# Waiting for the last zero fills on GpSimd instead of SyncE

## The chip, the cores and the metric

The kernel runs on one core of a Trainium2 chip. A core has five engines, each with its own instruction queue: TensorE (PE in the profile; its weight loads are PEld), VectorE (DVE), ScalarE (ACT), GpSimd (POOL) and SyncE (SP), which does not compute. SyncE, ScalarE and GpSimd issue the transfers, which 16 DMA engines carry out. Engines wait for each other and for transfers on semaphores. The metric is the device time of one execution in microseconds; lower is better.

## The reference

It is one decoder layer for one token with its backward pass: attention over a cached window, then a gated bilinear block, then the gradients of everything.

```python
W = min(4096, max(256, Sk // 4))                  # 4096 of Sk = 32768 cached rows
k = jnp.repeat(k_cache[:, :, Sk - W:, :], rep, axis=1)
v = jnp.repeat(v_cache[:, :, Sk - W:, :], rep, axis=1)
...
h = x + _A_ref(_layernorm(x, axis=-1), A_k_cache, A_v_cache, A_wq, A_wo)
h2 = h + _B_ref(_layernorm(h, axis=-1), B_w_gate, B_w_up, B_w_down)
...
_out, _vjp = jax.vjp(_f, A_x, A_k_cache, A_v_cache, A_wq, A_wo, B_w_gate, B_w_up, B_w_down)
_grads = _vjp(grad_out)
```

There are 8 key/value heads of 256 elements and 16 query heads. The gradients of the two caches (out_2 and out_3) have the full shape of the caches, 8 x 32768 x 256 in bfloat16, 134 MB each. Only the last 4096 rows of each head have a gradient; the 28,672 rows ahead of them are zero, and these zeros have to be written.

## The kernel before

The work has three stages. In the first, for each of the eight heads g, the kernel loads the window of keys and values, computes scores and softmax (`scores`) and sums of products (`moments`). The middle stage computes the output and the feed-forward block with its gradient. The last stage goes over the heads again in the order 6, 1, 3, 4, 5, 0, 7, 2 and computes the gradients of the window, which ScalarE's queue stores (L715); between the heads GpSimd computes the gradients of the weights (`outer`, L595, and `outer_B`, L632) and issues their stores. The last of these is the store of `job_qB` (L659), after which GpSimd has nothing but the program's end.

Beside this run the zero fills: 16 regions, one per head and cache, of 14,336 KB each (`regions`, L244). SyncE's queue (`ZQ`, L41) issues them. Two early ones read from the zeroed tile `pair` (L246); GpSimd waits for these (L248) before it loads over `pair`. The other 14 read from the tile `home` once VectorE has zeroed the rows that they use (`clear_rows`, L281). `fill_late` (L253) issues them, two at a time: a fill waits until the one before the last has landed, on one of two semaphores `zsem`. One region (`UNEVEN`) is split, and four of its pieces are issued by GpSimd, with a semaphore `psem` of their own. `fill_late` is called while head 1 of the first stage is traced (L401).

A framework called Tile orders each engine's instructions and sets the semaphores between them. The fills are kept out of its bookkeeping (`no_tile_sem_insts`, and the group "fills"), so the kernel waits for them itself: `fill_late` ends with waits of SyncE on `psem` and both `zsem` (L276 to L278), and the last of these waits is declared as the fence of the group (L279), the instruction that stands for the landing of all its members. `keep_in_program_order` pins an instruction behind what was traced before it on its engine.

When the context of the launch closes (L769), the program's end follows: SyncE waits for all semaphores of the framework, one instruction after another with up to two semaphores each, and drains; the other engines drain; GpSimd collects all of them in a barrier, clears the semaphores, and a second barrier ends the program.

Of the kernel before, what the change touches and what calls it, by code (L numbers as in the profile page):

```python
# [8 lines left out]
f32 = mybir.dt.float32  # L9
# [26 lines left out]
def kernel(  # L36
        ctx, tc, A_x, A_k_cache, A_v_cache, A_wq, A_wo, B_x, B_w_gate, B_w_up, B_w_down, grad_out,
           out_0, out_1, out_2, out_3, out_4, out_5, out_6, out_7, out_8):
    nc = tc.nc
    LD = nc.scalar  # L40
    ZQ = nc.sync  # L41

    const = ctx.enter_context(tc.tile_pool(name="const", bufs=1))
# [85 lines left out]
    nc.vector.memset(ones_bf[:], 1.0)  # L129
    ones_f = const.tile([128, 1], f32)  # L130
    nc.vector.memset(ones_f[:], 1.0)
    eps_t = const.tile([128, 1], f32)
    nc.vector.memset(eps_t[:], EPS)

# [66 lines left out]
    def load_kv(dst, cache, g, queue=LD):  # L201
        queue.dma_start(out=dst, in_=cache[0, g, Sk - W:, :].rearrange("(p t) d -> p t d", t=T))  # L202
# [32 lines left out]
    def rows_of(src, n):  # L235
        return src[0:128:4].unsqueeze(1).to_broadcast([32, n, src.shape[1]])

    def fill_with(dst, src, sem, group, queue=ZQ):
        fill = queue.dma_start(out=dst, in_=src)
        tc.info.no_tile_sem_insts.add(fill.ins.name)  # L240
        tc.add_to_no_dep_group(group, fill.ins)
        tc.keep_in_program_order(fill.then_inc(sem, 16))
# [10 lines left out]
    def fill_late():  # L253
        zsem = [tc.alloc_semaphore(f"zsem{j}") for j in range(DEEP)]
        psem = tc.alloc_semaphore("psem")
        due = [0] * DEEP
        for i, reg in enumerate(regions[EARLY:]):
            j = i % DEEP
            if i >= DEEP:
                tc.keep_in_program_order(ZQ.wait_ge(zsem[j], due[j]))  # L260
            n = NZ
            if i + EARLY == UNEVEN:
                odd = reg.rearrange("(r f) -> r f", f=ZW)[22 * 32:]
                reg = reg[0:22 * 32 * ZW]
                n = 22
                at = 0
                for e, base, rows, queue in ((3, 0, 8, nc.gpsimd), (2, 12, 2, nc.gpsimd), (3, 20, 13, nc.gpsimd), (8, 64, 13, nc.gpsimd), (4, 0, 5, ZQ), (1, 0, 1, ZQ)):
                    fill_with(odd[at:at + e * rows].rearrange("(e n) f -> e n f", e=e),
                              Z_late[base:base + 4 * e:4].unsqueeze(1).to_broadcast([e, rows, ZW]), zsem[j] if queue is ZQ else psem, "fills", queue)
                    at += e * rows  # L270
                    if queue is ZQ:
                        due[j] += 16
            for dst, src in [(reg.rearrange("(p n f) -> p n f", p=32, f=ZW), rows_of(Z_late, n))]:
                fill_with(dst, src, zsem[j], "fills")
                due[j] += 16
        tc.keep_in_program_order(ZQ.wait_ge(psem, 64))  # L276
        for j in range(DEEP):
            filled = tc.keep_in_program_order(ZQ.wait_ge(zsem[j], due[j]))  # L278
        tc.declare_fence(filled.ins, group="fills")  # L279

    def clear_rows():  # L281
        words = Z_late.bitcast(mybir.dt.int32)
        nc.vector.tensor_tensor(out=words, in0=words, in1=keep_i[:].to_broadcast([128, ZW // 2]), op=ALU.bitwise_and)
# [39 lines left out]
    with tc.tile_pool(name="ps_x", bufs=1, space=bass.MemoryType.PSUM) as ps_x, \  # L323
# [36 lines left out]
        def moments(g, p_f):  # L360
            K_sb, V_sb = K_of[g], V_of[g]
            if g < G - 1:
                M_t = ps_m.tile([128, 2, 2 * Dh], f32, tag="M", name="M_t")
                M_ps = [M_t[:, vh, :] for vh in range(2)]
            else:
                M_ps = [ps_tr.tile([128, 4, 128], f32, tag="tr", name="M_t")[:].rearrange("p t k -> p (t k)") for _ in range(2)]
            for c in range(8):
                pK = pK_slot[c % 2]
                for i in range(4):
                    t = 4 * c + i  # L370
                    for hh in range(2):
                        nc.vector.tensor_scalar(out=pK[:, i, hh, :], in0=K_sb[:, t, :], scalar1=p_f[:, 8 * i + c, hh:hh + 1], scalar2=None, op0=ALU.mult)  # L372
                for i in range(4):
                    t = 4 * c + i
                    for vh in range(2):
                        nc.tensor.matmul(M_ps[vh], lhsT=V_sb[:, t, vh * 128:(vh + 1) * 128], rhs=pK[:, i, :, :].rearrange("p h d -> p (h d)"),  # L376
                                         start=(t == 0), stop=(t == T - 1))
            for t in range(0, T, 4):
                for k in range(4):
                    tk, X_sb = t + 2 * (k // 2), (V_sb, K_sb)[k % 2]  # L380
                    nc.tensor.matmul(ok_ps[32 * k:32 * (k + 1), :], lhsT=ppad[g % 2][:, tk:tk + 2, :].rearrange("p t h -> p (t h)"),  # L381
                                     rhs=X_sb[:, tk:tk + 2, :].rearrange("p t d -> p (t d)"),
                                     start=(g == 0 and t == 0), stop=(g == G - 1 and t == T - 4))
            if g < G - 2:
                move_M(g, M_ps)
            else:
                M_late.append((g, M_ps))
# [7 lines left out]
        for g in range(G):  # L395
            p_f = p_next
            if g + 1 < G:
                p_next = scores(g + 1)
            if g == 1:
                clear_rows()  # L400
                fill_late()  # L401
            moments(g, p_f)
            for w, h in NEXT.get(g, ()):
                load_kv((K_of, V_of)[w][h], (A_k_cache, A_v_cache)[w], h)
            if g == G - 2:
                LD.dma_start(out=wo_sb[:, JW:], in_=wo_v[:, JW:])
                LD.dma_start(out=wd_sb, in_=wd_v[0])
# [23 lines left out]
    with tc.tile_pool(name="ps_mid", bufs=2, space=bass.MemoryType.PSUM) as ps_mid, \  # L431
# [76 lines left out]
        def close(dn, dcat):  # L508

            nc.vector.tensor_tensor(out=dn[:, 3:5], in0=dn[:, 3:5], in1=par_f[:], op=ALU.mult)  # L510
            nc.vector.tensor_copy(out=dcat[:, 0:3], in_=dn[:, 0:3])
            nc.vector.tensor_tensor(out=dcat[:, 3:4], in0=dn[:, 3:4], in1=dn[:, 4:5], op=ALU.add)
# [64 lines left out]
    with tc.tile_pool(name="work2", bufs=2) as work2, tc.tile_pool(name="lnw", bufs=1) as lnw, \  # L577
# [94 lines left out]
        for it, g in enumerate((6, 1, 3, 4, 5, 0, 7, 2)):  # L672
# [53 lines left out]
            if it == 6:  # L726
                dn1 = lnw.tile([128, 5], f32)
                for c, src, dq in ((0, wq2[0], dq_bc), (1, wq2[1], dq_bc), (2, wq2[2], dq_bc),
                                   (3, wqB, dq_bc[:, 0:HJ]), (4, wqB, dq_bc[:, HJ:2 * HJ])):
                    part = nc.vector.tensor_tensor_reduce(out=wq2[0][:, 0:src.shape[1]], in0=src, in1=dq, scale=1.0, scalar=0.0,  # L730
                                                          op0=ALU.mult, op1=ALU.add, accum_out=dn1[:, c:c + 1])
                    if c == 0:
                        tc.keep_in_program_order(part)
                dcat1 = lnw.tile([128, 8], f32)
                close(dn1, dcat1)
                dxT = layernorm_bwd(dcat1, xnT_f, rstd1, dhT[:], "ln1")
                dx_ps = ps_t.tile([1, D], f32, tag="tmp")
                for c in range(3):
                    nc.tensor.matmul(dx_ps[0:1, c * 128:(c + 1) * 128], lhsT=dxT[:, c:c + 1], rhs=ident_f[:], start=True, stop=True)
                nc.tensor.matmul(dx_ps[0:1, 384:D], lhsT=dxT[:, 3:4], rhs=pair_f[:], start=True, stop=True)  # L740
                dx_bf = x_bf
                nc.vector.tensor_copy(out=dx_bf[:, 0:384].rearrange("o (p c) -> o p c", c=3), in_=dx_ps[0:1, 0:384].rearrange("o (c p) -> o p c", c=3))
                nc.vector.tensor_copy(out=dx_bf[:, 384:D], in_=dx_ps[0:1, 384:D])
                LD.dma_start(out=out_1.rearrange("a b d -> (a b) d"), in_=dx_bf[:])

# [1 line left out]
_INS = ['A_x', 'A_k_cache', 'A_v_cache', 'A_wq', 'A_wo', 'B_x', 'B_w_gate', 'B_w_up', 'B_w_down', 'grad_out']  # L747
# [26 lines left out]
```

## Time and profile before

| | |
|---|---|
| median of 3 runs | 783.92 us (783.14 to 784.41) |
| the profiled execution: its time | 784.15 us |
| the profiled execution: span from first to last instruction | 782.4 us |
| bytes moved | 331.43 MB (50.43 MB read from HBM, 280.59 MB written to it) |
| mean rate over the span | 424 GB/s |
| busy share of PE, DVE, ACT, POOL | 57%, 49%, 25%, 24% |
| last issue of a fill by SyncE | 702.86 us |
| GpSimd's last issue (L659) | 682.97 us |
| ScalarE's last two stores (L715): start of the issues | 716.43 us |

The profile is one execution. Times count from the span's start. Digits in the page's slices are busy tenths of one fortieth of the span. A "q" behind an engine (SPq, POOLq) marks an instruction of its queue that waits, drains or issues and is not counted as busy. EVENT_SEMAPHORE is a wait on, or an update of, a semaphore; its start is the moment when the wait is over. DRAIN is the instruction with which an engine closes its work ahead of a barrier.

### The profile page before, as it was taken

The page shows a single profiled execution, that of the slowest core. Times are in us where ns is not written, and L with a number is a line of the kernel's source. Part 1 is how long each engine was busy: PE and PEld are TensorE (multiplying, and loading weights), DVE is VectorE, ACT ScalarE, POOL GpSimd, SP SyncE. Part 2 cuts the span into 40 slices and gives each one's busy share as a digit, 9 for nine tenths or more (in the row PEclk, how much of TensorE's full clock was granted, in tenths as well). Part 3 has the DMA queues.
Part 4 walks back from the last instruction along what each step waited for, and adds up shares of the span by engine and source line. Part 5 has one row for each costly group of instructions (what it writes and reads, how often), then busy time and mean ns, then how long its engine had stood idle before and what let it go on. Part 6 is the DMA issues. An engine that isn't in the chain of part 4 may idle for free.

```text
span 782.4 us, 6400 instructions
## 1 busy us (share of the span) xinstructions
PE 449.5 (57%) x2172; PEld 192.3 (25%) x2190; DVE 385.2 (49%) x1088; ACT 197.8 (25%) x309; POOL 190.2 (24%) x102
## 2 busy tenths in 40 slices
PE   1999999796889753313336985426888075021000
PEld 1444444242344321101122342112332031010000
DVE  8068655351178531142785284915675057964000
ACT  1442332334400000000111273405545045013000
POOL 7000001000000000000001977529194746900000
PEclk9999999899689956555557997556885567555555
DMA  9999999999999999999999999999999999999997
GB/s 375 431 420 431 427 436 417 426 430 427 431 428 423 427 428 429 430 429 430 432 432 433 428 426 427 427 410 428 432 415 427 417 431 432 430 431 426 430 428 327
DMA packets 23554, 331.43 MB, mean 424 GB/s; under 512 B 1758, under 2 KB 2786, under 8 KB 4802
## 3 DMA queue, kind: packets, MB, share of 16 engines
q1 hardware_dynamic: 14826, 250.43, 75.4%
q10 hardware_dynamic: 5176, 57.09, 17.2%
q0 software_dynamic: 3520, 23.51, 7.2%
q8 instruction: 17, 0.28, 0.1%
q14 instruction: 15, 0.12, 0.0%
HBM read 50.43 MB, written 280.59 MB: 423 GB/s over the span
## 4 chain that ended last, share of the span: by engine, by line
DMA 24%; PE 24%; DVE 18%; ACT 2%; issue 2%; DVEq 0%; ACTq 0%; POOLq 0%
DMA out_dram<-arena 11%; DMA arena<-in_B_w_up_dram 7%; DMA arena<-in_B_w_down_dram 4%; PE rows_ps L313 4%; PE M_t L376 4%; PE tr_ps L310 4%; PE d_ps L705 4%; DVE pair L730 3%; DMA arena<-in_A_k_cache_dram 2%; DVE arena L712 2%; DVE arena L713 2%; DVE arena L527 2%; PE dqb_ps L583 2%; DVE arena L471 2%; PE dqb_ps L589 1%
## 5 line engine op out<-in xcount | busy, mean ns | idle before, releaser
L372 DVE TENSOR_SCALAR arena<-arena,p_f 128x256 bf16<-128x256 bf16 x512 | 110.1, 280 | 34.1 <-PE tr_ps L310 16.1
L310 PE MATMUL tr_ps<-ident_f,arena 128*128 128x128 f32 x448 | 84.7, 319 | 44.7 <-DMA arena<-in_A_v_cache_dram 31.9
L313 PE MATMUL rows_ps<-arena,vpad 128*16 128x512 bf16 x256 | 88.9, 442 | 8.2 <-ACT arena L329 3.0
L329 ACT COPY arena<-tr_ps 128x1024 bf16<-128x1024 bf16 x64 | 63.6, 1013 | 83.8 <-PE tr_ps L310 82.1
L310 PEld LDWEIGHTS tr_ps<-ident_f,arena 128*128 128x128 f32 x448 | 56.2, 159 | 92.6 <-issue 64.5
L712 DVE CAST arena<-d_ps 128x512 bf16<-128x512 f32 x64 | 44.0, 688 | 67.3 <-PE d_ps L705 66.7
L376 PE MATMUL M_t<-arena 128*128 128x512 bf16 x308 | 75.2, 386 | 0.8 <-issue 0.2
L705 PE MATMUL d_ps<-arena 32*128 32x512 bf16 x256 | 46.8, 514 | 48.3 <-DVE arena L713 40.6
L709 ACT CAST arena<-d_ps 128x512 bf16<-128x512 f32 x64 | 37.9, 593 | 85.6 <-PE d_ps L705 81.7
L600 POOL TENSOR_SCALAR arena<-dh_bc,oX_f 128x448 bf16<-128x448 bf16 x32 | 44.9, 1412 | 28.8 <-DMA out_dram<-arena 28.6
L713 DVE CAST arena<-d_ps 128x512 bf16<-128x512 f32 x64 | 43.5, 680 | 13.8 <-DMA out_dram<-arena 13.8
L710 ACT CAST arena<-d_ps 128x512 bf16<-128x512 f32 x64 | 38.3, 599 | 23.8 <-DMA out_dram<-arena 23.8
L678 ACT COPY arena<-tr_ps 128x1024 bf16<-128x1024 bf16 x32 | 32.7, 1024 | 28.3 <-PE rows_ps L313 18.2
L376 PEld LDWEIGHTS <-arena 128*128 128x128 bf16 x320 | 30.2, 100 | 37.2 <-issue 7.1
L600 POOL TENSOR_SCALAR arena<-arena,xT 128x4096 bf16<-128x4096 bf16 x3 | 31.9, 10618 | 26.8 <-DMA out_dram<-arena 26.8
L315 DVE COPY arena<-rows_ps 16x512 f32<-16x512 f32 x16 | 10.8, 677 | 48.5 <-PE rows_ps L313 48.3
L417 POOL DMA_DIRECT2D arena<-in_A_wo_dram x1 | 0.6, 572 | 136.5 <-PE ok_ps L381 136.5
L482 PE MATMUL r_ps<-arena,X2pad 128*4 128x448 bf16 x24 | 10.4, 571 | 39.7 <-DMA arena<-in_B_w_up_dram 25.3
L600 POOL TENSOR_SCALAR arena<-pair,xT 128x1792 bf16<-128x1792 bf16 x6 | 28.7, 4794 | 12.7 <-DMA out_dram<-arena 12.6
L705 PEld LDWEIGHTS <-arena 32*128 32x128 bf16 x256 | 10.5, 96 | 86.8 <-DVE arena L713 41.8
L376 PE MATMUL M_t<-arena,pair 128*128 128x512 bf16 x124 | 29.5, 397 | 0.4 <-issue 0.2
L202 POOL DMA_DIRECT2D pair<-in_A_v_cache_dram x2 | 1.2, 629 | 114.5 <-POOLq L248 114.5
(240 smaller groups left out, 593.4 us busy)
## 6 DMA issues: line engine op xcount, KB each, us to landing
out_dram<-home SPq DMA_DIRECT2D x13, 14336.0 KB, 88.0
out_dram<-arena ACTq DMA_DIRECT2D x16, 2048.0 KB, 24.7
out_dram<-pair SPq DMA_DIRECT2D x2, 14336.0 KB, 93.5
out_dram<-home SPq DMA_DIRECT2D x1, 11264.0 KB
arena<-in_A_k_cache_dram ACTq DMA_DIRECT2D x5, 2048.0 KB, 21.5
arena<-in_A_k_cache_dram SPq DMA_DIRECT2D x3, 2048.0 KB, 19.7
arena<-in_A_v_cache_dram SPq DMA_DIRECT2D x3, 2048.0 KB, 30.0
arena<-in_A_v_cache_dram ACTq DMA_DIRECT2D x3, 2048.0 KB, 32.2
```

Of the source, the lines that this page charges most:

```text
L310: nc.tensor.transpose(tr_ps[:, i, :], X_sb[:, 4 * q + i, :].bitcast(f32), ident_f[:])
L313: nc.tensor.matmul(rows_ps[:], lhsT=pad[:, e, 16 * q:16 * q + 16], rhs=XT.rearrange("p (n e) -> p n e", e=2)[:, :, e], start=(q == 0 and e ...
L329: sT_ps = dots(K_of[g], KT_slot, vpad[g % 2], rows1, ps_c, "cols", lambda q, XT, ps: nc.scalar.copy(out=XT, in_=ps))
L372: nc.vector.tensor_scalar(out=pK[:, i, hh, :], in0=K_sb[:, t, :], scalar1=p_f[:, 8 * i + c, hh:hh + 1], scalar2=None, op0=ALU.mult)
L376: nc.tensor.matmul(M_ps[vh], lhsT=V_sb[:, t, vh * 128:(vh + 1) * 128], rhs=pK[:, i, :, :].rearrange("p h d -> p (h d)"), start=(t == 0), s ...
L600: nc.gpsimd.tensor_scalar(out=buf[:, off:off + n], in0=src, scalar1=col, scalar2=None, op0=ALU.mult)
L678: nc.scalar.copy(out=XT, in_=ps)
L705: nc.tensor.matmul(d_ps[:, qi].rearrange("p w d -> p (w d)"), lhsT=rm[32 * q:32 * (q + 1), l, :], rhs=Rs[32 * q:32 * (q + 1), :], start=Tr ...
L709: nc.scalar.copy(out=stV[:, t:t + 2, :], in_=d_ps[:, :, 0, :])
L710: nc.scalar.copy(out=stK[:, t:t + 2, :], in_=d_ps[:, :, 1, :])
L712: nc.vector.tensor_copy(out=stV[:, t:t + 2, :], in_=d_ps[:, :, 0, :])
L713: nc.vector.tensor_copy(out=stK[:, t:t + 2, :], in_=d_ps[:, :, 1, :])
```

## The change

A tile `done_t` of one element is added. `fill_late` no longer ends with the waits but returns its semaphores and the counts that they are to reach. A new function, `fills_done`, is called at the end of the kernel function, after all heads of the last stage. In it GpSimd waits on `psem` and both `zsem`, then sets `done_t` to zero, and this memset is declared as the fence. SyncE no longer waits for the last fills by an instruction of the kernel.

```diff
+    done_t = const.tile([1, 1], f32)
...
-        tc.keep_in_program_order(ZQ.wait_ge(psem, 64))
+        return zsem, psem, due
+
+    def fills_done(zsem, psem, due):
+        tc.keep_in_program_order(nc.gpsimd.wait_ge(psem, 64))
         for j in range(DEEP):
-            filled = tc.keep_in_program_order(ZQ.wait_ge(zsem[j], due[j]))
+            tc.keep_in_program_order(nc.gpsimd.wait_ge(zsem[j], due[j]))
+        filled = tc.keep_in_program_order(nc.gpsimd.memset(done_t[:], 0.0))
         tc.declare_fence(filled.ins, group="fills")
...
-                fill_late()
+                fill_sems = fill_late()
...
+        fills_done(*fill_sems)
```

## The prediction

> **What bounds the kernel now.** I read the page first, then the table by stretches of time, then SyncE's waits, then the instructions of the closing line. The page:
>
> ```profile
> span 782.4 us, 6400 instructions
> ...
> DMA  9999999999999999999999999999999999999997
> ...
> DMA packets 23554, 331.43 MB, mean 424 GB/s; under 512 B 1758, under 2 KB 2786, under 8 KB 4802
> ```
>
> The DMA engines are full in every slice but the last, while the busiest compute engine, PE, is busy for 57%. The kernel is 331.43 MB of transfers: 331.43 MB at 424 GB/s is 781.7 us, the whole span. So a change pays only if it moves bytes, or shortens what lies before the first or after the last of them. The end, by stretches (busy time and count of PE, PEld, DVE, ACT and POOL, then the clock, the DMA share and GB/s):
>
> ```profile
> 720.00:770.00 50.00, 0.00 (x0) 0.00 (x0) 0.00 (x0) 0.00 (x0) 0.00 (x0) 0.50 1.01 429
> 770.00:776.00 6.00, 0.00 (x0) 0.00 (x0) 0.00 (x0) 0.00 (x0) 0.00 (x0) 0.50 1.01 431
> 776.00:781.00 5.00, 0.00 (x0) 0.00 (x0) 0.00 (x0) 0.00 (x0) 0.00 (x0) 0.50 0.35 147
> 781.00:783.00 2.00, 0.00 (x0) 0.00 (x0) 0.00 (x0) 0.00 (x0) 0.00 (x0) 0.50 0.00 0
> ```
>
> From 720 us on no engine computes; the fills alone run, thin out from 776, and nothing moves after 781. What SyncE waits for, its last issue, and what runs on the program's closing line (duration in ns, then first and last start):
>
> ```profile
> SPq L239 <- DMA out_dram<-home: 576.7, 12, 76.7
> SPq L278 <- DMA out_dram<-home: 77.3, 2, 43.2
> ...
> 702.86 0.53 SPq L239 DMA_DIRECT2D out_dram<-home  x1
> ...
> L278 SPq EVENT_SEMAPHORE  x2: 17/22/28, 746.6 to 780.7; - x2
> ...
> L769 SPq EVENT_SEMAPHORE  x11: 17/28/28, 780.8 to 781.4; - x11
> L769 SPq DRAIN  x2: 7/10/13, 781.5 to 781.6; - x2
> ...
> L769 POOLq EVENT_SEMAPHORE  x2: 17/17/17, 781.6 to 781.7; - x2
> L769 POOLq DRAIN  x1: 18326/18326/18326, 682.9 to 682.9; - x1
> ```
>
> SyncE issues the last fill at 702.9, then stands in L278 until 780.7. Only then does it go through eleven waits and two drains (780.8 to 781.6), and GpSimd's barrier step at 781.6 follows them. GpSimd's own closing drain was over at 682.9 + 18.3 = 701.3; the drains of PE, DVE and ACT on that line started between 715.0 and 718.1. So between the last fill and the barrier only SyncE's list is on the path. The chain of waits on the page does not help here: it follows DVE's early drain and ends at 716.
>
> The views round these starts to a tenth; the trace's records hold them finer: last fill's semaphore 780.73, L278 released 780.74, first of the eleven waits 780.84, drains 781.51 and 781.57, GpSimd's step 781.60. So the path from last fill to barrier step is 0.87 us. Behind it stand the two barriers and GpSimd's clearing of semaphores (781.6 to 782.4), and 784.15 - 782.4 = 1.75 us outside the span; the change leaves both alone.
>
> **The change part by part.** The sum is made against the profiled execution, 784.15 us, which lies 0.23 above the median of 783.92 and inside the runs shown (783.14 to 784.41). I carry differences over to the median.
>
> *Removed from SyncE: the waits of L276 to L278.* Nothing but the closing line is queued behind them. Its eleven waits now run from about 703.4 on, while fills run for 77 us more: 780.74 to 781.51 leaves the path. Most of these waits are on semaphores long complete (the last store lands at 741.9); those not yet complete cost nothing before 780.
>
> *Added to GpSimd: the same waits and a memset of one element.* What is queued behind them is only GpSimd's closing drain and barrier steps: its last work is the issue at 683.0 (L659). No transfer and no other engine's work waits for that. All engines wait for GpSimd in the barrier, as before.
>
> *The new path from the last fill to GpSimd's barrier step.*
> - Release to memset: GpSimd operations that waited for a transfer (L600, L635) start 0.08 to 0.10 us after its semaphore by the records. If the last wait stays an instruction of its own, like L248 (17 ns), it is 0.02 more. I take 0.10.
> - The memset: four memsets at the start (L758) took 93 to 97 ns, the one of 128x128 283 ns. One element is nearest to the former: 0.09.
> - GpSimd's drain behind it: with nothing else in flight 40 and 113 ns here, 169 ns behind the four memsets, where it ended 0.05 after the last of them. It lies beside the next item: 0.
> - SyncE takes up the memset's count. In the records the drain at 781.51 is the instruction that names the semaphore of GpSimd's operations; none of the eleven waits does. So SyncE should stand in that drain already. A semaphore from one engine to another took 0.03 (SyncE's drain over at 781.58, GpSimd's step at 781.60), the second drain starts 0.06 after the first, and 0.03 again to GpSimd: 0.12 to 0.13.
>
> Sum 0.10 + 0.09 + 0.13 = 0.32 us, against 0.87: 0.55 us less. Profiled 783.6, at the median 783.4.
>
> Bounds of what the trace of before does not show. The shortest path is 0.08 + 0.09 + 0.12 = 0.29, a gain of 0.58. At the other end GpSimd's drain after the fills: the one of 18.3 us ended at 701.3, 1.1 us after its transfer landed (issue 682.97, 17.2 us to landing); if that 1.1 is always paid once GpSimd has issued transfers, the path is 0.10 + 0.09 + 1.12 + 0.04 = 1.35, 0.48 slower than now. I take the short drain, as nothing is in flight on GpSimd by 781.
>
> The Trainium skill's page "VectorE: DVE Perf Modes", section "The DRAIN you can't avoid", holds that the drains of the program's frame take a constant 12 ns or so on all five engines. This trace agrees for SyncE (7 to 13 ns) and not for GpSimd (40 to 18,326 ns). By that page the drain costs 0.01 instead of 0.05, beside the same 0.13 of SyncE, and the sum stays 0.32; by the long row it would be the first slow rival below, so the page speaks against that rival and the row keeps it alive.
>
> *done_t* takes four bytes per partition and moves the small tiles allocated after it. The transfers of the fills read pair and home, allocated before it: nothing.
>
> **The rivals.**
> - *SyncE stops too early*: its closing list meets GpSimd's count first, and all else comes after it. The change then doesn't do what it says: eleven waits at 0.06 (0.66) come back behind the memset, 0.32 + 0.66 = 0.98 against 0.87, 784.0 us. Against it: the drain, last in the list, holds that semaphore today. For it: the list is made anew and loses the count of SyncE's own last wait.
> - *GpSimd's drain is long* (slower): it is moved from 683, where 80 us of fills hide it, to the very end. If its 18.3 us are its price after transfers and not the wait for the transfer, the path is 0.10 + 0.09 + 18.33 + 0.04 = 18.56, 17.7 more: 801.6 us. For: the row. Against: it ended just after its transfer landed. It decides from a drain of about 2.3 us on; at 1.1 us it gives 784.4, no change.
> - *GpSimd takes up the memset slowly*, as it last ran one at 14.7 us. Rows: the first TENSOR_SCALAR after 66 us of waiting (L634) started 0.10 after its release, the first TENSOR_TENSOR (574.8) with no gap, and the longest delay after a release is 0.64 (L202's transfer). With 0.64 for 0.10 the path is 0.86, 783.9 us; it makes the kernel slower by 0.2% only from 2.2 us on. The Trainium skill's "GPSIMD Engine Reference", section "2.1 Instruction dispatch", gives about 6 us for the first call of a freshly loaded kernel; by it the sum would be 783.4 + 5.9 = 789.3 us, and no run here shows such a gap.
> - *The transfers end earlier* (faster): from 776 to 781 the DMA moves 147 GB/s x 5 us = 0.74 MB, which takes 1.7 us at 431 GB/s instead of 4.4 (to 780.4). If other addresses or another order of the engines evened out the end, 2.7 us more would go: 780.7 us. Nothing in the diff touches a fill; I find no step that leads there.
>
> **How the numbers follow.** From no change a measurement of this kernel can tell about 0.2%, 1.57 us; the runs of before alone lie 1.27 apart. The forecast (783.4) has 0.68; SyncE stopping early 0.10; a drain of 1.1 us 0.04; a long drain 0.05; a slow memset beyond 2.2 us 0.05; transfers ending earlier 0.08. Within 0.2% lie the first three: 0.82; slower 0.10; faster 0.08. The range takes the lowest run less the largest gain, 783.14 - 0.58 = 782.5 (rounded outward), to the highest run plus the longest bounded path, 784.41 + 0.48 = 784.9. It leaves out the three cases of the tails, 0.18.
>
> **What would show it.** Right: on the closing line SyncE's waits start near 703 and only its drains lie after 780; GpSimd shows a memset about 0.1 after the last fill, then a drain under 0.2; the span is near 781.9, and the last fill still lands near 780.7. Wrong: SyncE's waits again after 780 (stops early); a GpSimd drain of 1 us or more at the end; a gap of microseconds ahead of the memset; or the stretch 776 to 781 with another rate, in which case the time came from the transfers and not from the steps above.

## The result and the profile after

The changed kernel takes 785.64 us (median of 20 runs, 784.57 to 787.62); the kernel before took 783.96 us in 20 runs beside it. The ratio is 1.0024 with a 95% interval of 1.0017 to 1.0031: slower, by 1.3 to 2.4 us. The forecast was 783.4 us with a range up to 784.9.

The profiled execution took 784.85 us, with a span of 783.1. The page of the changed kernel shows the same transfers:

```profile
span 783.1 us, 6417 instructions
...
DMA  9999999999999999999999999999999999999997
...
DMA packets 23555, 331.43 MB, mean 423 GB/s; under 512 B 1759, under 2 KB 2787, under 8 KB 4803
```

The same stretches of time at the end:

```profile
720.00:770.00 50.00, 0.04 (x4) 0.00 (x0) 1.29 (x2) 1.07 (x2) 0.00 (x0) 0.50 1.01 428
770.00:776.00 6.00, 0.00 (x0) 0.00 (x0) 0.00 (x0) 0.00 (x0) 0.00 (x0) 0.50 1.01 429
776.00:781.00 5.00, 0.00 (x0) 0.00 (x0) 0.00 (x0) 0.00 (x0) 0.09 (x1) 0.50 0.35 151
781.00:783.00 2.00, 0.00 (x0) 0.00 (x0) 0.00 (x0) 0.00 (x0) 0.00 (x0) 0.50 0.00 0
```

The fills run as before (428 against 429 GB/s up to 770, 151 against 147 in the last stretch), and the sequence of operations on VectorE, ScalarE and GpSimd is the same but for the memset. The other engines' last operations reach a little past 720 in this execution. Of the 17 instructions more, 18 are matmul records that the trace of before lacks; GpSimd has two more instructions and SyncE three fewer. The last fill landed at 779.80 by the trace's records, 0.93 us earlier than in the profile before. That is scatter: over the profiles of this study the last fill landed between 779.58 and 781.99.

The closing line (L775 in the changed kernel) and the new wait and memset (L282, L283), by instruction, duration in ns, first and last start:

```profile
L775 SPq EVENT_SEMAPHORE  x10: 27/28/5956, 698.4 to 745.9; - x10
L775 SPq DRAIN  x2: 7/7/7, 780.1 to 780.1; - x2
...
L775 POOLq DRAIN  x1: 2327/2327/2327, 779.9 to 779.9; - x1
L775 POOLq EVENT_SEMAPHORE  x1: 17/17/17, 782.3 to 782.3; - x1
...
L282 POOLq EVENT_SEMAPHORE  x1: 43/43/43, 779.8 to 779.8; - x1
...
L283 POOL MEMSET done_t<- x1: 88/88/88, 779.9 to 779.9; 1x1 f32 x1
```

The change does what it says: ten of SyncE's waits lie between 698.4 and 745.9, and only its two drains come after the last fill, 0.26 and 0.32 us behind it (780.06 and 780.12). But GpSimd's drain stands there too, and it takes 2.33 us, from 779.93 to 782.26. GpSimd's barrier step follows at 782.30. The path from the last fill to that step is 782.30 - 779.80 = 2.50 us; before it was 0.87. The difference, 1.63 us, lies in the measured interval of 1.3 to 2.4.

### The profile page after: what moved, and what is told of

It reads as the page before. It is cut to its first block, busy times and chain, and to the rows that moved or that the text cites. A ratio compares the mean times of both kernels' runs of the same rounds, so it can differ in the third digit from the quotient of the medians.

```text
span 783.1 us, 6417 instructions
## 1 busy us (share of the span) xinstructions
PE 451.1 (58%) x2190; PEld 191.2 (24%) x2190; DVE 391.6 (50%) x1088; ACT 197.7 (25%) x309; POOL 191.5 (24%) x103
## 3 DMA queue, kind: packets, MB, share of 16 engines
q0 software_dynamic: 3520, 23.51, 7.2%
## 4 chain that ended last, share of the span: by engine, by line
DMA 29%; PE 27%; POOL 16%; another core or an unknown queue 12%; DVE 7%; issue 7%; ACT 1%; POOLq 0%; DVEq 0%; ACTq 0%
PE M_t L381 11%; DMA out_dram<-arena 11%; POOL arena L605 11%; DMA arena<-in_B_w_up_dram 7%; DMA arena<-in_B_w_down_dram 4%; PE rows_ps L318 4%; DMA arena<-in_A_v_cache_dram 4%; PE tr_ps L315 4%; DMA arena<-in_A_k_cache_dram 2%; DVE arena L532 2%; POOL arena L642 2%; PE ok_ps L386 2%; DVE arena L476 2%; POOL arena L640 1%
## 5 line engine op out<-in xcount | busy, mean ns | idle before, releaser
L315 PE MATMUL tr_ps<-ident_f,arena 128*128 128x128 f32 x448 | 82.9, 314 | 43.3 <-DMA arena<-in_A_v_cache_dram 30.2
L381 PE MATMUL M_t<-arena 128*128 128x512 bf16 x320 | 77.5, 387 | 0.6 <-DMA arena<-in_A_v_cache_dram 0.6
L315 PEld LDWEIGHTS tr_ps<-ident_f,arena 128*128 128x128 f32 x448 | 54.5, 156 | 89.6 <-issue 61.2
L717 DVE CAST arena<-d_ps 128x512 bf16<-128x512 f32 x64 | 45.0, 703 | 62.7 <-PE d_ps L710 62.5
L718 DVE CAST arena<-d_ps 128x512 bf16<-128x512 f32 x64 | 44.1, 690 | 15.3 <-DMA out_dram<-arena 15.3
L605 POOL TENSOR_SCALAR arena<-pair,xT 128x1792 bf16<-128x1792 bf16 x6 | 30.7, 5129 | 16.3 <-DMA out_dram<-arena 16.2
```

The source lines that it names most:

```text
L315: nc.tensor.transpose(tr_ps[:, i, :], X_sb[:, 4 * q + i, :].bitcast(f32), ident_f[:])
L605: nc.gpsimd.tensor_scalar(out=buf[:, off:off + n], in0=src, scalar1=col, scalar2=None, op0=ALU.mult)
L717: nc.vector.tensor_copy(out=stV[:, t:t + 2, :], in_=d_ps[:, :, 0, :])
L718: nc.vector.tensor_copy(out=stK[:, t:t + 2, :], in_=d_ps[:, :, 1, :])
```

## The experiments

**1. A drain of GpSimd ahead of its waits.**

```diff
     def fills_done(zsem, psem, due):
+        tc.keep_in_program_order(nc.gpsimd.drain())
         tc.keep_in_program_order(nc.gpsimd.wait_ge(psem, 64))
```

> The changed kernel with one more drain of GpSimd, put ahead of its three waits, right behind its last transfer (L659 of the kernel before). Theory A (the long closing drain is the price of the transfers that GpSimd issued since its last drain): the new drain takes about 18 us beside the fills, the closing drain after the fills takes 0.2 us or less instead of 2.33, the path from the last fill to GpSimd's barrier step is 0.3 to 0.4 us, and the time is about 0.5 below the kernel before (ratio 0.9993). Theory B (the memset is slow in GpSimd's cores and the drain waits for it): the closing drain stays at 2.3 us, ratio about 1.002. Theory C (GpSimd is slow in its first drain after a long idle time): the closing drain stays at 2.3 us, ratio about 1.002. Theory D (the first drain of the program's later part is slow because its code is not at hand): the closing drain is short, as under A.

The new drain (L280), and then what the closing line of this kernel holds between 780 and 781.25 us:

```profile
L280 POOLq DRAIN  x1: 17742/17742/17742, 682.6 to 682.6; - x1
...
L776 SPq DRAIN  x2: 7/10/13, 781.1 to 781.2; - x2
L776 POOLq DRAIN  x1: 176/176/176, 781.0 to 781.0; - x1
L776 POOLq EVENT_SEMAPHORE  x1: 17/17/17, 781.2 to 781.2; - x1
```

The new drain takes 17.74 us beside the fills, and the closing one falls from 2.33 to 0.18. The last fill landed at 780.87, the barrier step came at 781.23: 0.36 us. The time is 783.45 us (12 runs) against 784.32 for the kernel before, a ratio of 0.9987 [0.9978, 0.9997]. So the closing drain was the loss. Theory B and theory C fall: the memset is the same, and GpSimd stands idle as long (80 us from the end of the new drain to the last fill), yet the closing drain is short.

**2. The wait without the memset.**

```diff
         for j in range(DEEP):
-            tc.keep_in_program_order(nc.gpsimd.wait_ge(zsem[j], due[j]))
-        filled = tc.keep_in_program_order(nc.gpsimd.memset(done_t[:], 0.0))
+            filled = tc.keep_in_program_order(nc.gpsimd.wait_ge(zsem[j], due[j]))
```

> The changed kernel without the memset: GpSimd waits, and its last wait is itself the fence. Theory A (price of the transfers issued since the last drain): the closing drain still takes 2.2 to 2.4 us behind the wait, the time is that of the changed kernel, about 785.5. Theory B (the memset is slow): the closing drain falls to 0.2 us or less, the path from the last fill to GpSimd's barrier step to 0.3, the time to about 783.4. Theory C (idle time) and D (code not at hand): as A.

GpSimd's drains on this kernel's closing line:

```profile
L774 POOLq DRAIN  x3: 40/107/2197, 779.7 to 782.5; - x3
```

The first of the three takes 2.20 us with no memset ahead of it; the one execution took 784.5 us. The drain does not wait for the memset, apart from 0.13 us by which it is shorter here. Theory B falls a second time.

**3. VectorE in GpSimd's place.**

```diff
-        tc.keep_in_program_order(nc.gpsimd.wait_ge(psem, 64))
+        tc.keep_in_program_order(nc.vector.wait_ge(psem, 64))
...
-            tc.keep_in_program_order(nc.gpsimd.wait_ge(zsem[j], due[j]))
+            tc.keep_in_program_order(nc.vector.wait_ge(zsem[j], due[j]))
-        filled = tc.keep_in_program_order(nc.gpsimd.memset(done_t[:], 0.0))
+        filled = tc.keep_in_program_order(nc.vector.memset(done_t[:], 0.0))
```

> The changed kernel with VectorE in GpSimd's place: VectorE, which issues no transfers, has the three waits and the memset. All theories: GpSimd's closing drain lies at 683 to 701 again, beside the fills. A: VectorE's drain behind its memset is short (0.1 to 0.2 us), the path from the last fill to GpSimd's barrier step is 0.1 (release) + 0.1 (memset) + 0.2 (the last steps of SyncE's list behind VectorE's count) + 0.1 = 0.5 us against 0.87, ratio about 0.9995. Theory C (an engine's first drain after a long idle time is slow, on any engine): VectorE's drain takes microseconds and the ratio is 1.001 or more. If the time comes from the transfers and not from the closing line (theory E), the ratio stays near 1.002.

VectorE's drain behind its memset, and GpSimd's drains:

```profile
L775 DVEq DRAIN  x1: 95/95/95, 781.3 to 781.3; - x1
...
L775 POOLq DRAIN  x3: 40/104/18054, 682.7 to 782.1; - x3
```

VectorE, idle since 716, drains in 0.1 us, and GpSimd's long drain is back beside the fills. The last fill landed at 781.16 and GpSimd's step came at 781.64: 0.48 us, as expected. The time is 784.30 us (12 runs), ratio 0.9997 [0.9987, 1.0008]. The path is 0.4 us shorter than before, which this measurement can't tell from none; but the loss of the change is gone.

**4 to 6. How many transfers stand between two drains.** Each of three kernels has one drain of GpSimd more, ahead of one of its transfers: ahead of the last one (L659 of the kernel before), ahead of the first store of `job_gB` (L646), and ahead of the load of wo (L417). The diff shows the first of them.

```diff
+                tc.keep_in_program_order(nc.gpsimd.drain())
-                nc.gpsimd.dma_start(out=out4_B, in_=buf[:, 0:HJ])
+                tc.keep_in_program_order(nc.gpsimd.dma_start(out=out4_B, in_=buf[:, 0:HJ]))
```

> The changed kernel with a drain of GpSimd just ahead of its last transfer, so that exactly one transfer is issued between that drain and the closing one; the last store is issued some 15 us later, beside the fills. Theory A with a price per drain: the closing drain still takes about 2.3 us. Theory A with a price per transfer (26 or so of them before): it falls to some 0.2 us. Theory B (memset) and C (idle time): 2.3 us. Theory D (code of the drain not at hand): short, 0.2 us or less.

> The changed kernel with a drain of GpSimd ahead of the first transfer of job_gB, so that 8 of GpSimd's 26 transfers are issued between that drain and the closing one; GpSimd stands still there until its earlier transfers land, some 10 us in the middle of the last stage. Two closing drains measured so far: 2.33 us behind 26 transfers, 0.18 behind none, so 0.083 us for one transfer if the price is per transfer. Theory A per transfer: 0.18 + 8 x 0.083 = 0.84 us. Theory A per descriptor: these 8 transfers have about 38% of the data descriptors, 1.0 us. Theory D (the code of the drain is not at hand unless a drain ran before): 0.2 to 0.3 us.

> The changed kernel with a drain of GpSimd ahead of the load of wo (L417 of the kernel before), so that 20 of GpSimd's 26 transfers follow it. Theory A per transfer: the closing drain takes 0.18 + 20 x 0.083 = 1.8 us. Theory A per descriptor (84% of them): 2.0 us. Theory D: 0.2 to 0.3 us.

GpSimd's drains on the closing lines of the three kernels; the longest of each row is the one behind the memset:

```profile
L776 POOLq DRAIN  x3: 46/104/268, 779.8 to 780.6; - x3
```

```profile
L777 POOLq DRAIN  x3: 46/113/837, 779.9 to 781.3; - x3
```

```profile
L776 POOLq DRAIN  x3: 46/113/1822, 780.4 to 782.8; - x3
```

With 1, 8 and 20 transfers since the drain before, the closing drain takes 0.27, 0.84 and 1.82 us. The first run alone could still be read as theory D (a first drain is slow because its code is not at hand), but in all three a drain had run before, and the price rises with the number of transfers: theory D falls. The single executions took 782.66, 783.34 and 784.80 us. In the first, the last store was issued at 685.93, 3 us later than in the kernel before and not the 15 that I had expected.

I had expected 38% and 84% of the descriptors behind the drains of the second and third kernel. By the packets on GpSimd's queue in their traces it is 28% (992 of 3520) and 74%, and a price by the packet would give 0.79 and 1.76 us. That is too near to the measured 0.84 and 1.82 to tell number from packets; the next two runs do.

**7 and 8. Number, packets or pieces.** Both add a drain behind GpSimd's last store, and then extra loads into a dead buffer ahead of the waits: 24 loads of 16 bytes, or one load in 2048 pieces of 16 bytes.

```diff
+        tc.keep_in_program_order(nc.gpsimd.drain())
+        parts = wst[wst_ctr[0] % 2][0:1]
+        for k in range(24):
+            tc.keep_in_program_order(nc.gpsimd.dma_start(out=parts[:, 8 * k:8 * k + 8], in_=A_x[0, :, 8 * k:8 * k + 8]))
```

```diff
+        tc.keep_in_program_order(nc.gpsimd.drain())
+        parts = wst[wst_ctr[0] % 2][:, 0:256].rearrange("p (a b) -> p a b", b=16)
+        tc.keep_in_program_order(nc.gpsimd.dma_start(out=parts[:, :, 0:8], in_=A_wq[0:128, 0:256].rearrange("p (a b) -> p a b", b=16)[:, :, 0:8]))
```

> The kernel with a drain of GpSimd behind its last store, and then 24 more loads on GpSimd's queue, each of 16 bytes into a dead buffer, ahead of the three waits. They land long before the last fill. Theory A per transfer: the closing drain takes 0.18 + 24 x 0.083 = 2.2 us. Theory A per descriptor: these loads have few, 0.3 to 0.5 us. Theory D: 0.2 us.

> The kernel with a drain of GpSimd behind its last store, and then one more load on GpSimd's queue in 2048 pieces of 16 bytes into a dead buffer, ahead of the three waits. Theory A per transfer: the closing drain takes 0.18 + 0.083 = 0.26 us. Theory A per descriptor: 2048 pieces against the 3520 packets of GpSimd's 26 transfers, 0.18 + 2.15 x 0.58 = 1.4 us. Theory D: 0.2 us. The small pieces cost the DMA engines some microseconds, so the whole time may be longer; the closing drain is what is read here.

The closing drains, of the kernel with 24 tiny loads first:

```profile
L779 POOLq DRAIN  x1: 2139/2139/2139, 782.1 to 782.1; - x1
```

```profile
L778 POOLq DRAIN  x3: 46/104/266, 780.5 to 781.3; - x3
```

24 loads of 16 bytes cost 2.14 us, between the 1.82 of 20 and the 2.33 of 26 of the kernel's own transfers. They are 768 packets (4288 on GpSimd's queue against 3520); priced by the packet, at (2.33 - 0.18) / 3520 us each, they would have cost 0.65 us. One load of 2048 pieces costs 0.27, as one store did. My expectation for it set its pieces against packets, which are not the same thing: the 2048 pieces went in 48 packets. So this run rules out a price by the piece, and the run before it a price by the packet. The time since the drain before is ruled out too: the closing drain began 85 us after it with the tiny loads and 80 us after it with the one load. What counts is the number of transfers that GpSimd issued (all rows with the memset; without it, 26 transfers cost 2.197 us):

| transfers since the drain before | closing drain, us | 0.18 + 0.0826 x number |
|---|---|---|
| 0 (two runs) | 0.176, 0.178 | 0.18 |
| 1 (two runs: a store, the load in 2048 pieces) | 0.268, 0.266 | 0.26 |
| 8 | 0.837 | 0.84 |
| 20 | 1.822 | 1.83 |
| 24 (the tiny loads) | 2.139 | 2.16 |
| 26 (the changed kernel, two runs) | 2.327, 2.328 | 2.33 |

The drain that experiment 5 has in the middle of the kernel gives one more point. The 18 transfers ahead of it had landed by 571.01, GpSimd's last operation ahead of it ended at 572.22, and the drain ended at 573.79, 1.57 us later. The closing drains behind no transfer ended 0.07 us after the memset, and 0.07 + 18 x 0.0826 = 1.56. So the price is not one of the program's end.

The execution with the tiny loads took 786.88 us; its last fill landed at 781.99, later than in any other profile. One execution can't tell whether the loads held up the fills.

**9 and 10. The changed kernel and the drain ahead of its waits, on one chip.**

> The changed kernel as it is, on the same chip as the next run. The closing drain of 2.3 us makes the path from the last fill to GpSimd's barrier step 2.5 us against 0.88, 1.6 us more: ratio 1.0021. If more than the closing line is slower (theory E, transfers), the ratio lies clearly above that, 1.003 or more.

> The changed kernel with a drain of GpSimd ahead of its waits, for a second time and on the same chip as the changed kernel: path from the last fill to the barrier step 0.36 us against 0.88, 0.5 us less than the kernel before, ratio 0.9993, and 2.1 us less than the changed kernel. If the first run's 0.9987 was no accident and something beyond the closing line gains, the ratio is 0.9987 or less again.

The closing drains of the two, the changed kernel first:

```profile
L775 POOLq DRAIN  x3: 40/113/2328, 780.0 to 782.9; - x3
```

```profile
L776 POOLq DRAIN  x3: 34/104/178, 780.0 to 780.8; - x3
```

The changed kernel: 786.16 us (6 runs), ratio to the kernel before 1.0027 [1.0015, 1.0040]. With the drain ahead of the waits: 783.27 us (11 runs), 0.9995 [0.9987, 1.0004]. The paths from the last fill to the barrier step are 2.50 and 0.35 us in these profiles. The expected ratios, 1.0021 and 0.9993, lie in both intervals, so nothing beyond the closing line is needed to explain either; the medians of 2.9 us apart are more than the 2.15 us of the paths, within their scatter.

The version with the drain ahead of the waits has the shortest path of those tried. The path is 0.5 us shorter than that of the kernel before in both profiles. One of its two intervals lies wholly below 1, the other holds 1; a gain of 0.07% is at the edge of what these runs can tell.

## Why the prediction was wrong

*The bound.* Right: the transfers set the time, and the rates of the last stretches are unchanged. What the change was worth had to come from the path behind the last fill, and all of it did.

*Removed from SyncE.* Right: its waits moved ahead of the fills' end. The rival that SyncE would stop early at GpSimd's count did not come: the drain, last in its list, holds that count.

*Release to memset, and the memset.* Release 779.80, memset 779.95 to 780.04: 0.15 and 0.09 against 0.10 and 0.09. The slow restart did not come either: the memset started 0.15 us after the release, though GpSimd had last run one at 14.7 us. The 6 us that the Trainium skill gives for the first call of a freshly loaded kernel ("GPSIMD Engine Reference", section "2.1 Instruction dispatch") do not appear in this trace.

*SyncE takes up the count.* Right in size: memset over at 780.04, SyncE's drains at 780.06 and 780.12. With the short drain of experiment 1 the whole path is 0.36 us, against the 0.32 of the sum.

*GpSimd's drain behind it: "It lies beside the next item: 0".* This is the step that failed. It measured 2.33 us and is the longest piece of the new path. I had three drains of 0.04 to 0.17 us and one of 18.3 us, and took the short ones because nothing would be in flight on GpSimd by 781. That nothing of GpSimd's is in flight is true (its last transfer landed at 704.3 in the changed kernel's profile), and it is not what the drain depends on: it pays 0.083 us for each of the 26 transfers issued since the drain before, long landed or not. The short drains of the kernel before all had no transfer between them and the drain before them; the long one had all 26. The drain covers the memset and SyncE's two steps, so they drop out of the sum: 0.13 from the release to the drain, 2.33 for the drain, 0.04 from its end to GpSimd's step, 2.50 us in all. The time is then 783.92 - 0.87 + 2.50 = 785.55 us; 785.64 was measured. A drain of 1 us or more at the end was also among the signs of being wrong that I had named.

The bound for this item was wrong too. I read 1.1 us from the long drain, the time by which it outlasted its last transfer. It was no upper bound: the same 26 transfers cost 2.33 us where all had landed before the drain began. I read this as work that the drain does while it waits for a transfer; the traces show only the times. The rival with the long drain had the right place, and I gave it 0.05; its price of 18.3 us was eight times too high. That the drain came out at the 2.3 us from which this rival was to decide is luck. By the rival's own terms that point is 2.2 us (0.87 + 1.57 - 0.10 - 0.09 - 0.04), and nothing in my working led to a drain of that length.

By the rule that I set beside the row, drains of the program's frame take a constant 12 ns or so on all engines (the Trainium skill, "VectorE: DVE Perf Modes", section "The DRAIN you can't avoid"). SyncE's agree with it (7 to 13 ns); GpSimd's measured 40 to 2,327 ns behind the fills, and there the measurement decides.

## What to carry to other kernels

When a wait moves from one engine to another, what the new engine still has to do behind it moves onto the path, its closing drain included; look at how long that drain takes where it stands now, and ask what it pays for before calling it short. In these runs the better places for the last wait were VectorE, which issues no transfers, and GpSimd once it had drained. And when a row offers two prices 100 times apart for one instruction, find what differs between the instances (here: transfers issued since the drain before) before choosing the nearer-looking one.

## What the runs showed of the hardware

GpSimd's closing drain costs 0.18 us behind a small memset plus 0.083 us for each transfer that GpSimd issued since its last drain. In these runs it made no difference whether a transfer moved 16 bytes or 2 MB, in how many packets or pieces, or how long ago it had landed: the last one landed 38 to 83 us before the closing drain, the first were issued up to 650 us before it, and the drain in the middle of experiment 5 paid the same 1.2 us after its last landing.

Where the drain has to wait for a transfer, it ends sooner after the landing than that: behind 26 transfers 1.12 us after the last one landed (experiment 1: landed 699.24, over at 700.35), behind the first 6 transfers 0.30 us (experiment 6: landed 202.80, over at 203.10), about half the price by the number. What the drain does for each transfer, the traces do not show.

SyncE and ScalarE do not pay this in the kernel before. SyncE's first closing drain, behind 27 transfers of its own that had all landed, took 13 ns. ScalarE's, behind 37, took 0.15 us and was over at 718.27, although ScalarE's last store landed only at 741.89.
